# Sparse attention with a soft mixture of experts: three of four q/k strips loaded in 1 KB rows by one transfer each, and a new order of steps

## The chip, the cores and the metric

The kernel runs on one core of one Trainium2 chip. The metric is device time in microseconds (us). Before the change three runs gave 279.32, 279.91 and 282.58 us; the median is 279.91 us. The profiled execution is one more run, at 283.02 us. Granted TensorE clock is given as a share of 2.4 GHz; 0.5 means 1.2 GHz.

## The reference

Eight batches, eight heads, 576 tokens, head size 64, all float32. Heads 0 to 3 see a window of 32 tokens ("local"), heads 4 to 7 the tokens with the same position modulo 32 ("strided"). The attention's output, with heads side by side, goes through a soft mixture of 8 experts with 4 slots each.

```python
mask_local = (rel >= 0) & (rel < 32)
mask_strided = (rel >= 0) & (pos[None, :] % 32 == pos[:, None] % 32)
scores = np.where(masks[None], q @ k.transpose(0, 1, 3, 2) / np.sqrt(D), -1e9)
attn_out = softmax(scores) @ v                   # [8, 8, 576, 64]
x = attn_out.transpose(0, 2, 1, 3).reshape(4608, 512)
logits = x @ phi                                 # [4608, 32]
slot_input = softmax(logits, axis=0).T @ x       # [32, 512]
slot_out[e] = relu(slot_input[e] @ w1[e]) @ w2[e]
out = softmax(logits, axis=1) @ slot_out
```

## The kernel before

**Stages.** The kernel has an attention loop of 16 steps, then a drain and the tail. Step `i` treats batch `i // 2`, and in it two local heads (suffix L) and two strided heads (suffix S). The tail brings in what is left of the expert weights, runs the experts, and stores the output.

**Loads of a step.** Queries and keys of the tokens 64 to 575 come as four strips, kL, qL, kS and qS, each of two heads, 256 KB. `emit_D` issues them on SP's queue. The strip qL is one transfer (line 290): partition p holds four tokens of each head, so that a packet is 1 KB and all 128 partitions are written. The strips kL, kS and qS are two transfers of 128 KB each (line 294): a head has 64 partitions, and each partition holds eight tokens, a packet of 2 KB. The first 64 tokens of all heads (`Dt`, line 299, every second step) and the values (`Dv`, lines 304 and 307, and `Ds`, line 312) are further transfers. Of the 64 blocks of expert weights (512 KB each, line 244 and others) 30 are issued inside the loop (`w`).

**Buffers.** `nat` gives a strip its place: four slots of `natb`, used in turn in the canonical order kL, qL, (t), kS, qS. A load must therefore wait until the load four places earlier has been read by TensorE (or by POOL, which reads qL). The values of the strided heads, `vs`, have one buffer.

**DMA lanes.** The transfers on SP take eight completion semaphores in turn. Each transfer waits until the one eight places before it has landed, so no more than eight are under way.

**Transposes.** `turn` (line 328) transposes four blocks of 128 columns of a strip on TensorE into a PSUM bank, and `emit_e` copies the bank to the tiles `kLb`, `kSb` or `qtb` on ScalarE, with an access pattern that puts tokens in order. For qL, POOL first sorts the strip into `nat2` (`emit_g`, line 323), so that a block holds both heads. In kL, kS and qS a block is a pair of tokens by 64 dimensions, for both heads.

**Order.** Every step has a name (`TkL` transposes kL, `ekL` copies it out, `SL` and `SS` are scores, `a`, `m`, `b`, `EX`, `s` the softmax, `P` and `f` its transposition, `AL` and `AS` the products with values, `X`, `x`, `LG` the later parts) and a number in the table `PHASE`. Step `n` of `i` is emitted at `10 * i + PHASE[n]`; all are sorted by this, and each engine runs its own in that order. Suffixes y and z give numbers of their own to the first and the last `i`.

Of the kernel before, what the change touches and what calls it, by code (L numbers as in the profile page):

```python
# [25 lines left out]
TN = 4  # L26
NI = 36
# [3 lines left out]

PER = 10.0
PHASE = dict(
    Tt=0.3822, et=1.7933, kcL=2.2893, kcS=4.2207, gqL=0.1069, TkL=-4.3302, ekL=-0.8212, TqL=0.1189, eqL=2.3418,
    TkS=0.0364, ekS=4.2997, TqS=1.7301, eqS=2.355, SL=3.2822, SS=6.7794, a2=11.0625, aA=7.9078, a1=7.1235, m2=12.4254,
    m1=8.3441, b2=12.5475, b1=9.6628, EX2=14.022, EX1=11.0057, PA=14.416, fA=16.5383, PL=13.9339, fL=17.5174,
    s2=14.5712, s1=16.4348, rc=17.1249, PS=15.0921, fS=16.9509, AL=19.132, AA=22.0385, nA=23.9111, nL=21.817,
    AS=18.6462, nS=20.038, XS=21.78, xS=23.3769, XL=23.6524, xL=25.5687, XB=24.899, xB=27.8377, LG=27.6985,
    lc=29.6796, T9=24.5604, x9=25.9634, G9=27.1881, lg=29.1761, c9=28.3874, bm=29.2468, ED=29.6763, E9=30.4064,
    EA=29.7637, DT=31.1019, dt=31.2401, zz=32.7907, z9=34.5183, SI=31.8402, S9=32.9908, ac=33.8253, Dt=-4.4167,  # L40
    DkL=-9.127, DqL=-5.5006, DkS=-6.0373, DqS=-4.2053, C2=15.0077, Dv=6.1895, Ds=13.7301, zv=6.3414, SI0=1321.5679,
    S90=1379.9589, SI1=1483.7422, S91=1849.8957, mt=1013.1477, gm=1105.8595, wP=1174.6367, wD=1189.6775, wA=1214.8774,
    zD=1813.3179, zP=2101.5254, rg=2466.7324, ac0=1559.8399, ac1=1877.0405, ms=806.9735, sP0=1634.1847, sD0=1697.2594,
    sP1=2131.0366, sD1=2592.0768, Px=1984.3327, P0=2005.0906, P1=2790.0989, P2=3007.9876, P3=3368.8942, P4=3371.9343,
    P5=3376.775, P6=3689.0133, Dsz=7.9979, DkLz=-6.1029, TkLz=-0.7073, ekLz=3.1899, DqLz=-2.2526, gqLz=3.4277,
    TqLz=7.3306, eqLz=11.7249, DkSz=-8.1864, TkSz=3.3797, ekSz=11.8909, DqSz=-2.1099, TqSz=0.552, eqSz=13.2762,
    kcLz=11.4872, kcSz=10.0958, Dvz=6.9716, C2z=22.07, SLz=12.2707, SSz=13.3533, PAz=288.7773, PLz=321.7366,
    PSz=332.7395, ALz=375.9609, AAz=370.9401, ASz=519.1193, XSz=707.4419, XLz=681.9619, XBz=879.7536, LGz=878.9582,
    T9z=542.7143, G9z=780.8206, DTz=1138.1211, a1z=27.7962, aAz=61.8185, a2z=97.8287, m1z=168.544, m2z=240.9994,
    b1z=208.4859, b2z=261.8524, s1z=294.2249, s2z=308.0275, rcz=328.4212, nSz=697.2792, nLz=530.3168, nAz=475.5805,  # L50
    lgz=900.9235, c9z=787.6677, bmz=934.8942, zzz=1638.7908, z9z=1684.8229, dtz=1148.8275, EX1z=232.6822,
    EX2z=295.8221, fAz=353.4314, fLz=373.5109, fSz=464.8821, xLz=790.8422, xSz=825.6899, xBz=1452.5598, x9z=753.5728,
    EDz=951.8699, E9z=1093.3994, EAz=1408.0027, b9=29.2094, U9=31.8282, u9=32.068, b9z=859.2151, U9z=1267.3242,
    u9z=1341.0063, sw=1523.0731, DkLy=0.0, TkLy=4.4344, ekLy=6.2962, DqLy=-1227.8995, gqLy=-1040.3093, TqLy=-785.3182,
    eqLy=-726.4301, DkSy=-652.0224, TkSy=-612.1271, ekSy=-108.6268, DqSy=-568.916, TqSy=-177.1509, eqSy=-41.0303,
    Dty=-856.1564, Tty=-773.837, ety=-262.108, kcLy=-40.1673, kcSy=-257.5721, Dvy=3.2651, Dsy=8.1858, C2y=15.6738,
    SLy=6.2994, SSy=5.8701, PAy=15.183, PLy=16.1105, PSy=12.2748, ALy=22.3281, AAy=19.7659, ASy=19.3498, XSy=21.7384,
    XLy=25.1438, XBy=26.4902, LGy=28.9777, a1y=9.6423, aAy=8.0076, a2y=6.401, m1y=10.5053, m2y=7.5658, b1y=11.8225,
    b2y=8.6715, s1y=15.3267, s2y=13.3513, rcy=17.4693, nSy=20.9998, nLy=22.8474, nAy=24.2303, EX1y=13.9196,
    EX2y=10.8774, fAy=17.2098, fLy=18.5321, fSy=18.2348, xLy=27.1116, xSy=24.1831, xBy=30.3395, lcy=31.6159, Dw=12.0,  # L60
    Dx=148.0,
)

SEQ = "eehhllllllllsrtrorrorrorrstOOOfff"
# [26 lines left out]
def tile_sparse_attention_soft_moe(  # L91
# [39 lines left out]
    kLb, kSb = big("kLb", 2 * S), big("kSb", 2 * S)  # L131
# [26 lines left out]
    kt = {"kL": kLb, "kS": kSb, "qL": qtb[:, 0:512], "qS": qtb[:, 512:1024]}  # L158
# [18 lines left out]
    x9 = x9b.rearrange("p (c d) -> p c d", c=4)  # L177
# [20 lines left out]
    def give(t):  # L198
# [166 lines left out]
    def emit_kc(s, i):  # L365

        for a in range(2):
            h = slice(64 * a, 64 * a + 64)
            src = tl[h, i % 2 + (2 if s == "S" else 0), 0]
            PC(out=kL[h, a, 0:64] if s == "L" else kA[h, a], in_=src)  # L370
            if s == "S":
                for n in range(2):
                    dst = kSb[64 * n:64 * n + 64].rearrange("d (j h m x) -> d j h m x", h=2, m=2, x=2 * NI)[:, :, a, :, NI * n:NI * n + 4]
                    PC(out=dst, in_=src.rearrange("d (i m j n) -> d j m i n", i=4, m=2, n=2)[:, :, :, :, n])

    def score(t, c, x, wd, lhsT, rhs):
        nc.tensor.matmul(out=t[0][32 * c:32 * c + 32, x:x + wd], lhsT=lhsT, rhs=rhs, start=True, stop=True, skip_group_check=True)  # L377
# [20 lines left out]

    def part(t, which):
# [279 lines left out]
    for s in "LS":  # L679
# [168 lines left out]
    for a in range(2):  # L848
        r = slice(64 - 64 * a, 128 - 64 * a)
# [181 lines left out]
```

## Time and profile before

| | |
|---|---|
| median of three runs | 279.91 us |
| profiled execution | 283.02 us, of which the span from the first to the last instruction is 281.2 us |
| TensorE (PE) busy | 229.4 us, 82% of the span |
| VectorE (DVE) busy | 168.5 us, 60% |
| ScalarE (ACT) busy | 154.0 us, 55% |
| GpSimd (POOL) busy | 83.3 us, 30% |
| DMA | 72.80 MB, mean 259 GB/s; the main queue's packets fill 89.7% of the 16 engines' time |
| chain that ended last | PE 40%, DMA 34%, SP's queue 10% |

Busy times of TensorE are modelled from pipelined matmuls and say little about how much room it has; the gaps between its instructions say more. DMA share is the mean busy share of the 16 DMA engines. The chain is followed back from the last instruction, at each step to what released it. "SPq" is SP's queue issuing a transfer.

### The profile page before, as it was taken

Reading aid. Unit: us, or ns where it says so; the run is one execution under the profiler, and the core shown is the slowest. Engines: PE = TensorE matmul, PEld = TensorE weight load, DVE = VectorE, ACT = ScalarE, POOL = GpSimd, SP = SyncE. Lnnn points to the kernel's source line nnn. Section 1 sums busy time; section 2 is a strip of 40 time slices with the busy share of each in tenths; the row PEclk is TensorE's granted clock in tenths of the full one; section 3 lists DMA queues with packets and bytes.
Section 4 is the critical chain, followed back from the end, with each engine's and each line's share of the span. In section 5 each row is a group of like instructions: output and inputs, shape, how many; then the busy total and the mean of one; then the engine's idle time right before and its main releaser. Section 6 shows DMA issues by size and latency. Waiting matters only on the chain.

```text
span 281.2 us, 9759 instructions
## 1 busy us (share of the span) xinstructions
PE 229.4 (82%) x3974; PEld 173.1 (62%) x3974; DVE 168.5 (60%) x376; ACT 154.0 (55%) x342; POOL 83.3 (30%) x187
## 2 busy tenths in 40 slices
PE   7967797969889597979995999949888999898600
PEld 3755676758668486957983988839674335455400
DVE  5166756865687577668972787845867731035700
ACT  2575847759666665955984598635642114034600
POOL 5262452515246042414705331435210200000000
PEclk9999999999999999998996899987999999999965
DMA  7779999899888999999979968993899999988996
GB/s 180 183 233 235 253 233 239 260 206 281 211 240 228 224 268 226 230 267 260 226 226 243 242 193 250 258 266 95 294 377 393 362 409 325 280 277 288 340 291 264
DMA packets 64813, 72.80 MB, mean 259 GB/s; under 512 B 34048, under 2 KB 48768, under 8 KB 64768
## 3 DMA queue, kind: packets, MB, share of 16 engines
q1 hardware_dynamic: 63808, 71.85, 89.7%
q8 instruction: 31, 0.51, 0.8%
q10 hardware_dynamic: 960, 0.33, 0.6%
q14 instruction: 14, 0.11, 0.2%
HBM read 62.72 MB, written 9.44 MB: 257 GB/s over the span
## 4 chain that ended last, share of the span: by engine, by line
PE 40%; DMA 34%; SPq 10%; issue 4%; DVE 4%; ACT 1%; POOL 1%; DVEq 0%; POOLq 0%; ACTq 0%
DMA natb<-in_q_dram 14%; DMA wb<-in_moe_w_dram 12%; PE bank L328 6%; PE bank L459 5%; DMA vs<-in_v_dram 5%; PE bank L807 4%; PE bank L507 4%; SPq L294 4%; PE bank L377 4%; PE bank L649 3%; PE bank L922 3%; DMA natb<-in_k_dram 2%; PE bank L451 2%; PE bank L947 2%; SPq L304 1%
## 5 line engine op out<-in xcount | busy, mean ns | idle before, releaser
L328 PE MATMUL bank<-cf,natb 128*128 128x128 f32 x280 | 43.7, 291 | 18.4 <-DMA natb<-in_q_dram 8.5
L328 PEld LDWEIGHTS bank<-cf,natb 128*128 128x128 f32 x280 | 31.9, 147 | 29.0 <-issue 8.9
L416 DVE TENSOR_TENSOR pb<-bank,cb 128x288 f32<-128x288 f32 (+2 forms) x48 | 22.6, 474 | 21.7 <-PE bank L377 16.7
L323 POOL COPY natb<-natb 128x512 f32<-128x512 f32 x16 | 9.9, 619 | 80.8 <-DMA natb<-in_q_dram 42.1
L489 DVE TENSOR_TENSOR xnb<-bank,rz 128x512 f32<-128x512 f32 (+1 forms) x33 | 22.0, 669 | 9.6 <-PE bank L459 9.5
L344 ACT COPY kLb<-bank 64x256 f32<-64x256 f32 x64 | 25.3, 395 | 2.6 <-PE bank L377 1.3
L377 PE MATMUL bank<-kLb,qtb 128*32 128x128 f32 x576 | 25.5, 281 | 0.0
L459 PE MATMUL bank<-vs,ptb 128*32 128x128 f32 x480 | 16.4, 274 | 10.5 <-DMA vs<-in_v_dram 5.8
L428 ACT ACTIVATE pb<-pb 128x288 f32<-128x288 f32 (+1 forms) x32 | 19.2, 599 | 7.7 <-DVE pb L424 7.1
L424 DVE TENSOR_TENSOR pb<-pb,mx 128x288 f32<-128x288 f32 (+1 forms) x32 | 22.1, 692 | 0.9
L421 DVE TENSOR_REDUCE mx<-pb 128x8 f32<-128x288 f32 (+1 forms) x32 | 21.8, 681 | 0.6
L431 DVE TENSOR_REDUCE rz<-pb 128x8 f32<-128x288 f32 (+1 forms) x32 | 20.6, 685 | 2.2 <-ACT pb L428 1.7
L507 PE MATMUL bank<-cf,xnb 128*128 128x128 f32 x128 | 21.6, 297 | 0.0
L455 ACT COPY ptb<-bank 128x512 f32<-128x512 f32 x32 | 17.4, 589 | 6.6 <-PE bank L451 5.3
L377 PEld LDWEIGHTS bank<-kLb,qtb 128*32 128x32 f32 x576 | 18.0, 113 | 4.6 <-issue 3.4
L459 PEld LDWEIGHTS bank<-vs,ptb 128*32 128x32 f32 x480 | 13.2, 109 | 12.3 <-ACT kLb L344 4.8
L451 PE MATMUL bank<-cf,pb 128*128 128x128 f32 x128 | 19.6, 278 | 0.0
L351 ACT COPY kSb<-bank 64x512 f32<-64x512 f32 x32 | 18.4, 575 | 1.5 <-PE bank L328 1.1
L318 POOL COPY vb<-vb 64x1024 f32<-64x1024 f32 x16 | 16.6, 1037 | 8.0 <-DMA vb<-in_v_dram 2.7
L459 PE MATMUL bank<-vb,ptb 128*32 128x128 f32 x512 | 17.8, 273 | 0.1
L507 PEld LDWEIGHTS bank<-cf,xnb 128*128 128x128 f32 x128 | 15.9, 152 | 2.5 <-DVE x9b L499 1.0
L338 ACT COPY qtb<-bank 128x512 f32<-128x512 f32 x16 | 9.4, 587 | 14.4 <-PE bank L328 14.4
(173 smaller groups left out, 468.5 us busy)
## 6 DMA issues: line engine op xcount, KB each, us to landing
wb<-in_moe_w_dram SPq DMA_DIRECT2D x48, 512.0 KB
natb<-in_k_dram SPq DMA_DIRECT2D x70, 128.0 KB
natb<-in_q_dram SPq DMA_DIRECT2D x38, 128.0 KB
vb<-in_v_dram SPq DMA_DIRECT2D x32, 144.0 KB
vs<-in_v_dram SPq DMA_DIRECT2D x30, 144.0 KB
natb<-in_q_dram SPq DMA_DIRECT2D x16, 256.0 KB
out_dram<-wb SPq DMA_DIRECT2D x16, 256.0 KB
vb<-in_moe_w_dram SPq DMA_DIRECT2D x4, 512.0 KB
```

Source lines behind the costliest of these rows:

```text
L328: nc.tensor.transpose(out=t[0][:, 128 * n:128 * n + 128], in_=src[:, 128 * n:128 * n + 128], identity=ident)
L344: ACT(out=dst.rearrange("d (p j n) -> d p j n", j=4, n=2)[:, :, :, n], in_=t[0][64 * n:64 * n + 64].rearrange("d (j h p) -> d p j h", j=4, ...
L377: nc.tensor.matmul(out=t[0][32 * c:32 * c + 32, x:x + wd], lhsT=lhsT, rhs=rhs, start=True, stop=True, skip_group_check=True)
L416: nc.vector.tensor_tensor(out=dst, in0=src, in1=mk.rearrange("p (s k) -> p s k", s=n).unsqueeze(3).to_broadcast([P, n, kk, 2]), op=ALU.add)
L421: nc.vector.tensor_reduce(out=part(box[i][0], w), in_=psg[w].rearrange("p s k a -> p s a k"), op=ALU.max, axis=AX.X)
L424: nc.vector.tensor_tensor(out=psg[w], in0=psg[w], in1=over(box[i][0], w), op=ALU.subtract)
L428: nc.scalar.activation(out=t, in_=t, func=AF.Exp, scale=0.125)
L431: nc.vector.tensor_reduce(out=part(box[i][1], w), in_=psg[w].rearrange("p s k a -> p s a k"), op=ALU.add, axis=AX.X)
L451: nc.tensor.transpose(out=t[0][:, 128 * r:128 * r + 128], in_=pb[:, lo + 128 * r:lo + 128 * r + 128], identity=ident)
L459: nc.tensor.matmul(out=t[0][32 * c:32 * c + 32, 128 * r:128 * r + 128], lhsT=lhsT, rhs=rhs, start=True, stop=True, skip_group_check=True)
L489: nc.vector.tensor_tensor(out=xn[:, place(i, s), r0:r0 + nr].rearrange("p r (a d) -> p r a d", a=2), in0=t[0][:, 128 * r0:128 * r0 + 128 * ...
L507: nc.tensor.transpose(out=t[0][:, 128 * r:128 * r + 128], in_=xn[:, place(i, s), r, :], identity=ident)
```

## The change

The three strips kL, kS and qS get the layout of qL: partition p holds four tokens of each of both heads, in packets of 1 KB over all 128 partitions, and one transfer of 256 KB brings them. Their blocks of 128 columns are now pairs of tokens of one head; nothing is sorted, and the copies out of PSUM, the small copies of `emit_kc` and the index in `emit_SS` follow the new places. The strip qL still goes through POOL's sort. All numbers of the table `PHASE` are new.

```diff
-    Tt=0.3822, et=1.7933, kcL=2.2893, kcS=4.2207, gqL=0.1069, TkL=-4.3302, ekL=-0.8212, TqL=0.1189, eqL=2.3418,
+    Tt=-2.0579, et=-0.6655, kcL=0.1445, kcS=1.0426, gqL=-4.396, TkL=-6.6862, ekL=-3.8918, TqL=-3.1071, eqL=-1.5805,
...
         src = (k if x[0] == "k" else q)[i // 2, heads(i, x[1]), 64:]
-        if x == "qL":
-            nc.sync.dma_start(out=nat(x, i).rearrange("p (h x) -> p h x", h=2), in_=src.rearrange("h (p n) d -> p h (n d)", n=TN))
-        else:
-
-            for h in range(2):
-                nc.sync.dma_start(out=nat(x, i)[64 * h:64 * h + 64], in_=src[h].rearrange("(p n) d -> p (n d)", n=8))
+        nc.sync.dma_start(out=nat(x, i).rearrange("p (h x) -> p h x", h=2), in_=src.rearrange("h (p n) d -> p h (n d)", n=TN))
...
-                    ACT(out=dst.rearrange("d (p j n) -> d p j n", j=4, n=2)[:, :, :, n],
-                        in_=t[0][64 * n:64 * n + 64].rearrange("d (j h p) -> d p j h", j=4, h=2)[:, :, :, a])
+                    ACT(out=dst.rearrange("d (p j n) -> d p j n", j=2, n=2)[:, :, :, n],
+                        in_=t[0][64 * n:64 * n + 64].rearrange("d (h j p) -> d p j h", j=2, h=2)[:, :, :, a])
         elif x == "qS":
-            ACT(out=kt[x].rearrange("d (x m i) -> d x m i", m=2, i=32), in_=t[0].rearrange("d (x i m) -> d x m i", i=32, m=2))
+
+            ACT(out=kt[x].rearrange("d (x m i) -> d x m i", m=4, i=32), in_=t[0].rearrange("d (x i m) -> d x m i", i=32, m=4))
...
-                    y = 2 * c + z
-                    x = 4 * (y % 4) + 2 * h + y // 4
+                    x = 8 * h + 4 * z + c
                     score(t, c, 128 + 2 * NI * (2 * h + z), 2 * NI, kt["qS"][:, 32 * x:32 * x + 32], kSb[:, 2 * NI * x:2 * NI * x + 2 * NI])
```

SP's queue, from the values of group 4 to a weight block, in the kernel before. Line 312 is `Ds4`, line 294 with `in_k` is kS of group 6, line 290 its qL, line 299 the first tokens, line 294 with `in_q` its qS, line 304 `Dv5`. The words in brackets are what the transfer waits for; "DMAHW" with a number is a lane.

```order
L312 DMA vs<-in_v_dram 36x1024 [waits DMAHW7_49,PE_49]
L312 DMA vs<-in_v_dram 36x1024 [waits DMAHW0_49]
L294 DMA natb<-in_k_dram 64x512 [waits DMAHW1_49,PE_49]
L294 DMA natb<-in_k_dram 64x512 [waits DMAHW2_49]
L290 DMA natb<-in_q_dram 128x2x256 [waits DMAHW3_49,Pool_49]
L299 DMA natb<-in_k_dram 64x8x64 [waits DMAHW4_49]
L299 DMA natb<-in_q_dram 64x8x64 [waits DMAHW5_49]
L294 DMA natb<-in_q_dram 64x512 [waits DMAHW6_49,PE_49]
L294 DMA natb<-in_q_dram 64x512 [waits DMAHW7_49]
L304 DMA vb<-in_v_dram 64x9x64 [waits DMAHW0_49]
L304 DMA vb<-in_v_dram 64x9x64 [waits DMAHW1_49]
L244 DMA wb_96<-in_moe_w_dram 128x1024 [waits DMAHW2_49]
```

The same place of SP's queue after the change, one group of strips later in the list (group 7: kL, `Ds5`, a weight block, then qL, kS and qS, then `Dv6`). Line 288 is a whole strip.

```order
L288 DMA natb<-in_k_dram 128x2x256 [waits DMAHW6_49,Pool_49]
L306 DMA vs<-in_v_dram 36x1024 [waits DMAHW7_49,PE_49]
L306 DMA vs<-in_v_dram 36x1024 [waits DMAHW0_49]
L243 DMA wb_97<-in_moe_w_dram 128x1024 [waits DMAHW1_49]
L288 DMA natb<-in_q_dram 128x2x256 [waits DMAHW2_49]
L288 DMA natb<-in_k_dram 128x2x256 [waits DMAHW3_49]
L288 DMA natb<-in_q_dram 128x2x256 [waits DMAHW4_49,PE_49]
L298 DMA vb<-in_v_dram 64x9x64 [waits DMAHW5_49,PE_49]
L298 DMA vb<-in_v_dram 64x9x64 [waits DMAHW6_49]
```

A strip is one row instead of two, so the lanes come round after fewer strips; qL now stands ahead of kS, and `Ds` ahead of the weight block that it followed.

TensorE's order in the middle of a step before the change, from the transposition of qS (line 328) over `XS` (507), `SI` (649), `AA` (459), `SL` (377), `XL` (507), `PL` (451), `PA` (440), `XB` (528) and `PS` (451) to that of the next kL.

```order
L328 MATMUL bank_124<-cf,natb 128x128 x4
L507 MATMUL bank_120<-cf,xnb 128x128 x4
L649 MATMUL bank_121<-xnb,dt 32x256 x8
L459 MATMUL bank_119<-vb 32x128 x4
L377 MATMUL bank_117<-kLb,qtb 32x128 x16
L507 MATMUL bank_122<-cf,xnb 128x128 x4
L451 MATMUL bank_123<-cf,pb 128x128 x4
L440 MATMUL bank_124<-cf,pb 128x128
L528 MATMUL bank_120<-cf,xtb 128x128 x4
L451 MATMUL bank_121<-cf,pb 128x128 x4
L328 MATMUL bank_119<-cf,natb 128x128 x4
```

The same stretch after the change; 501 is now the line of `XS` and `XL`, 322 of the strips, 643 of `SI`, 453 of `AA`, 372 of `SL`, 445 of `PL` and `PS`, 522 of `XB`, 434 of `PA`.

```order
L501 MATMUL bank_118<-cf,xnb 128x128 x4
L322 MATMUL bank_123<-cf,natb 128x128 x4
L643 MATMUL bank_120<-xnb,dt 32x256 x8
L453 MATMUL bank_124<-vb 32x128 x4
L372 MATMUL bank_121<-kLb,qtb 32x128 x16
L445 MATMUL bank_119<-cf,pb 128x128 x4
L501 MATMUL bank_117<-cf,xnb 128x128 x4
L445 MATMUL bank_122<-cf,pb 128x128 x4
L522 MATMUL bank_118<-cf,xtb 128x128 x4
L322 MATMUL bank_120<-cf,natb 128x128 x4
L434 MATMUL bank_124<-cf,pb 128x128
```

The same instructions stand in both; neighbours have changed places: qS after `XS`, `PL` ahead of `XL`, `PS` ahead of `XB`, `PA` behind the next kL.

## Rows read from the trace of the kernel before

**Rows 1.** Windows: stretch, its length, busy us per engine, clock, DMA share, GB/s.

```profile
20.00:180.00 160.00, 137.67 (x2721) 116.27 (x2722) 112.08 (x248) 110.05 (x247) 62.60 (x145) 0.97 0.95 239
180.00:200.00 20.00, 16.35 (x315) 14.17 (x317) 12.29 (x27) 10.54 (x24) 8.36 (x14) 0.83 0.73 199
200.00:232.00 32.00, 28.73 (x351) 14.71 (x343) 21.60 (x59) 9.13 (x22) 2.93 (x3) 1.00 0.99 381
```

**Rows 2.** Chain that ended last, from 20 to 190 us, shares by line.

```profile
by line: DMA natb<-in_q_dram 19.2%; DMA wb<-in_moe_w_dram 12.7%; PE bank L328 8.6%; DMA vs<-in_v_dram 7.5%; PE bank L459 6.2%; PE bank L377 5.9%; PE bank L507 5.6%; issue 4.8%; SPq L294 4.5%; DMA natb<-in_k_dram 4.1%; PE bank L649 3.9%; PE 
```

**Rows 3.** Pieces of that chain and of its start: start us, length us, what.

```profile
12.56 3.16 DMA natb<-in_q_dram
...
39.15 7.34 DMA wb<-in_moe_w_dram
...
51.63 6.69 DMA wb<-in_moe_w_dram
...
87.89 7.63 DMA wb<-in_moe_w_dram
95.58 0.50 SPq L294
```

**Rows 4.** TensorE's timeline over two steps: start, us, operation, idle time before it.

```profile
88.87 1.06 PE L377 MATMUL bank<-kLb,qtb 128*32 128x128 f32 x32
...
96.79 1.08 PE L459 MATMUL bank<-vs,ptb 128*32 128x128 f32 x32 [3.14 <-ACT pb L428]
...
100.59 0.63 PE L328 MATMUL bank<-cf,natb 128*128 128x128 f32 x4 [0.28 <-DMA natb<-in_q_dram]
...
108.93 1.08 PE L459 MATMUL bank<-vs,ptb 128*32 128x128 f32 x32 [1.44 <-ACT kLb L344]
...
111.98 1.09 PE L328 MATMUL bank<-cf,natb 128*128 128x128 f32 x8 [0.51 <-POOL natb L323]
...
113.68 1.06 PE L377 MATMUL bank<-kLb,qtb 128*32 128x128 f32 x32
```

**Rows 5.** SP's issues by line: duration ns min/median/max, first and last start.

```profile
L294 SPq DMA_DIRECT2D natb<-in_k_dram x62: 465/594/2179, 5.3 to 177.2; - x62
L290 SPq DMA_DIRECT2D natb<-in_q_dram x16: 427/527/1814, 0.7 to 181.5; - x16
```

**Rows 6.** SP's timeline: start, us for all of a row, transfer.

```profile
0.74 0.45 SPq L290 DMA_DIRECT2D natb<-in_q_dram  x1
...
5.32 3.05 SPq L294 DMA_DIRECT2D natb<-in_k_dram  x4
...
14.29 1.66 SPq L312 DMA_DIRECT2D vs<-in_v_dram  x2
...
226.91 15.48 SPq L256 DMA_DIRECT2D wb<-in_moe_w_dram  x8
```

**Rows 7.** Windows where one kind of transfer runs (columns as in rows 1).

```profile
7.00:9.00 2.00, 2.00 (x9) 1.47 (x9) 0.00 (x0) 0.59 (x1) 0.44 (x3) 1.00 0.93 246
...
236.00:238.00 2.00, 2.00 (x41) 1.23 (x44) 0.43 (x1) 0.61 (x2) 0.00 (x0) 1.00 0.97 326
238.00:240.00 2.00, 2.00 (x44) 1.23 (x40) 0.00 (x0) 0.00 (x0) 0.00 (x0) 1.00 0.99 305
```

**Rows 8.** SP's waits: who waited for whom, us in total, times, longest.

```profile
SPq L294 <- DMA wb<-in_moe_w_dram: 5.5, 5, 1.6
```

**Rows 9.** Groups by line: busy us, mean ns of one, idle us before and who ended it.

```profile
L323 POOL COPY natb<-natb 128x512 f32<-128x512 f32 x16 | 9.9, 619 | 80.8 <-DMA natb<-in_q_dram 42.1 <-PE bank L459 21.2 <-DMA vb<-in_v_dram 6.4
...
L347 ACT COPY qtb<-bank 128x512 f32<-128x512 f32 x16 | 9.5, 592 | 4.3 <-PE bank L328 4.2
L338 ACT COPY qtb<-bank 128x512 f32<-128x512 f32 x16 | 9.4, 587 | 14.4 <-PE bank L328 14.4
```

More of the change, by code (lines that the diff above doesn't have):

```diff
@@ L33 @@
 PHASE = dict(
-    Tt=0.3822, et=1.7933, kcL=2.2893, kcS=4.2207, gqL=0.1069, TkL=-4.3302, ekL=-0.8212, TqL=0.1189, eqL=2.3418,
[L35 to L58, printed above, removed]
@@ L59 @@
-    b2y=8.6715, s1y=15.3267, s2y=13.3513, rcy=17.4693, nSy=20.9998, nLy=22.8474, nAy=24.2303, EX1y=13.9196,
-    EX2y=10.8774, fAy=17.2098, fLy=18.5321, fSy=18.2348, xLy=27.1116, xSy=24.1831, xBy=30.3395, lcy=31.6159, Dw=12.0,
-    Dx=148.0,
+    Tt=-2.0579, et=-0.6655, kcL=0.1445, kcS=1.0426, gqL=-4.396, TkL=-6.6862, ekL=-3.8918, TqL=-3.1071, eqL=-1.5805,
+    TkS=-2.8079, ekS=0.2405, TqS=-1.638, eqS=2.0281, SL=0.8447, SS=4.3002, a2=4.9137, aA=5.6049, a1=4.0131, m2=9.2207,
+    m1=7.9989, b2=10.3387, b1=8.4466, EX2=10.6844, EX1=9.7238, PA=13.5374, fA=17.3669, PL=12.8131, fL=15.0172,
@@ new lines @@
+    s2=12.3728, s1=10.9688, rc=12.5764, PS=12.8393, fS=13.2679, AL=16.6069, AA=20.3205, nA=21.9987, nL=20.3493,
+    AS=15.8184, nS=18.2514, XS=18.3058, xS=21.1039, XL=22.8265, xL=22.9517, XB=23.0972, xB=27.0486, LG=25.4195,
+    lc=28.2806, T9=23.2544, x9=24.5474, G9=25.2863, lg=26.0999, c9=25.9908, bm=26.6978, ED=26.9719, E9=27.6734,
+    EA=28.1908, DT=27.3659, dt=28.3798, zz=29.6743, z9=30.6305, SI=30.0667, S9=30.5273, ac=31.1579, Dt=-5.774,
+    DkL=-9.8545, DqL=-6.5505, DkS=-6.2446, DqS=-5.1332, C2=13.94, Dv=5.3521, Ds=10.9507, zv=9.5434, SI0=1233.6152,
@@ new lines @@
+    S90=1337.0003, SI1=1340.2779, S91=1792.2637, mt=1006.8642, gm=1224.659, wP=1232.9455, wD=1351.0811, wA=1457.2594,
+    zD=1674.8517, zP=2208.5085, rg=3431.8563, ac0=1540.6421, ac1=1908.4892, ms=1369.382, sP0=1599.2965, sD0=1636.4837,
+    sP1=2063.102, sD1=2063.7014, Px=1936.2395, P0=1956.3048, P1=2242.6644, P2=2744.3559, P3=3051.4956, P4=3384.7871,
+    P5=4048.1529, P6=4135.3064, Dsz=10.4973, DkLz=-14.2155, TkLz=-3.0006, ekLz=8.8872, DqLz=1.1442, gqLz=4.0624,
+    TqLz=8.953, eqLz=10.94, DkSz=-10.8748, TkSz=-3.877, ekSz=-1.7646, DqSz=-7.0334, TqSz=1.8577, eqSz=6.1303,
@@ new lines @@
+    kcLz=1.2757, kcSz=0.4144, Dvz=3.6518, C2z=471.0423, SLz=11.0707, SSz=10.5949, PAz=396.9704, PLz=458.8301,
+    PSz=519.4974, ALz=589.7334, AAz=551.4381, ASz=603.3993, XSz=714.4744, XLz=685.0062, XBz=965.6281, LGz=774.6018,
+    T9z=667.5722, G9z=730.2393, DTz=1063.5269, a1z=159.2114, aAz=122.2744, a2z=91.9546, m1z=210.8829, m2z=271.9005,
+    b1z=240.0783, b2z=315.4588, s1z=397.8074, s2z=434.2949, rcz=475.8997, nSz=667.9874, nLz=643.2038, nAz=593.3993,
+    lgz=966.0232, c9z=730.9931, bmz=995.0075, zzz=1381.7738, z9z=1523.0304, dtz=1228.5284, EX1z=327.7961,
@@ new lines @@
+    EX2z=346.6191, fAz=414.1154, fLz=476.6392, fSz=551.6975, xLz=699.8901, xSz=756.0396, xBz=1328.1133, x9z=680.0565,
+    EDz=1017.2556, E9z=1047.5151, EAz=1358.9622, b9=26.413, U9=30.0178, u9=30.0947, b9z=792.3005, U9z=1160.7289,
+    u9z=1264.6704, sw=1495.1309, DkLy=0.0, TkLy=0.282, ekLy=1.1911, DqLy=-1954.5694, gqLy=-1013.5182, TqLy=-708.2666,
+    eqLy=-330.8771, DkSy=-1033.3414, TkSy=-455.8707, ekSy=-317.8524, DqSy=-435.3099, TqSy=-270.9075, eqSy=-233.4198,
+    Dty=-1569.5444, Tty=-714.8319, ety=-474.0413, kcLy=-54.7535, kcSy=-144.5437, Dvy=2.0079, Dsy=0.5923, C2y=14.7865,
@@ L62 @@
+    SLy=4.7404, SSy=0.3891, PAy=13.5974, PLy=13.6588, PSy=10.7209, ALy=18.5353, AAy=16.8047, ASy=16.3107, XSy=21.3403,
+    XLy=26.5822, XBy=26.0313, LGy=29.2819, a1y=8.6685, aAy=8.1403, a2y=1.3758, m1y=9.2843, m2y=5.5075, b1y=9.4624,
+    b2y=6.6793, s1y=11.0301, s2y=13.7963, rcy=14.228, nSy=17.5206, nLy=21.4472, nAy=24.8177, EX1y=9.84, EX2y=7.1264,
+    fAy=15.7781, fLy=15.6772, fSy=12.598, xLy=26.792, xSy=24.9093, xBy=34.1502, lcy=30.3079, Dw=12.0, Dx=148.0,
 )
@@ L350, in emit_e @@
                 r = slice(64 * n, 64 * n + 64)
-                ACT(out=kt[x][r].rearrange("d (x m n i) -> d x m n i", m=2, n=2, i=NI)[:, :, :, n, 4:],
-                    in_=t[0][r].rearrange("d (x i m) -> d x m i", i=32, m=2))
+                ACT(out=kt[x][r].rearrange("d (x m n i) -> d x m n i", m=4, n=2, i=NI)[:, :, :, n, 4:],
+                    in_=t[0][r].rearrange("d (x i m) -> d x m i", i=32, m=4))
         give(t)
@@ L372, in emit_kc @@
                 for n in range(2):
-                    dst = kSb[64 * n:64 * n + 64].rearrange("d (j h m x) -> d j h m x", h=2, m=2, x=2 * NI)[:, :, a, :, NI * n:NI * n + 4]
-                    PC(out=dst, in_=src.rearrange("d (i m j n) -> d j m i n", i=4, m=2, n=2)[:, :, :, :, n])
+                    dst = kSb[64 * n:64 * n + 64].rearrange("d (h j m x) -> d h j m x", h=2, m=4, x=2 * NI)[:, a, :, :, NI * n:NI * n + 4]
+                    PC(out=dst, in_=src.rearrange("d (i m j n) -> d j m i n", i=4, m=4, n=2)[:, :, :, :, n])
     def score(t, c, x, wd, lhsT, rhs):
```

## Prediction

> **What bounds the kernel now.** I read the windows by stage first. From 20 to 180 us the 16 DMA engines are 0.95 busy and yet move only 239 GB/s, while the same engines carry 381 GB/s from 200 to 232 us, where only weight blocks run [rows 1]. So the loop keeps the queues full with transfers that go slowly. In the chain of waits inside the loop (20 to 190 us, 170 us long) the four DMA entries make 19.2 + 12.7 + 7.5 + 4.1 = 43.5%, 74 us, and SP's issuing at line 294 another 4.5%, 7.7 us [rows 2]. No engine alone is the bound: TensorE's timeline shows why. From one `SL` to the second next one, 88.87 to 113.68 us, two steps take 24.8 us, 12.4 each, and the gaps before instructions add up to 3.14 + 0.28 + 1.44 + 0.51 = 5.4 us [rows 4]. TensorE's own work is thus 19.4 us, 9.7 a step; 2.7 us a step are waits. SP is nearly as full: a step has 14.9 issues on average (k and q strips 7, values 4, first tokens and their values 2, weights 30/16 = 1.9), and at 0.53 to 0.59 us each [rows 5] that is 8 to 9 of 12.4 us. The loop is a coupling of three nearly full resources, and the transfers are the slowest of them.
>
> After the loop the weight stretch is DMA at 0.99 [rows 1]. Its blocks wait for buffers that the last steps set free, so it starts when the loop ends and keeps its length; what the loop gains, the end gains.
>
> **The change, part by part.**
>
> *Rate of the strips.* Of the 64 strips 48 change layout. Between 7 and 9 us the queues carry nearly nothing but strips in halves (the four halves issued from 5.32 us on, and those ahead of them [rows 6]), at 0.93 share and 246 GB/s [rows 7]: 262,144 bytes take 1.07 us. Packets of 1 KB over all partitions run alone from 236 to 240 us, the last weight blocks, issued at line 256 [rows 6], at 326 and 305 GB/s [rows 7]: 0.83 us. That is 0.235 us saved per strip. Five strips lie in the start-up; 43 x 0.235 = 10.1 us of queue time in the loop. How much of it reaches the end? All, if the queues bind everywhere: −10.1. If only the part of the chain that runs through DMA shrinks, 43.5%: −4.4. The share of 0.95 speaks for the first, the 57% of the chain outside DMA for the second; neither is nearer, so I take the middle, **−7.3**.
>
> The Trainium skill speaks on both sides here. Its page "DMA: Bandwidth & Descriptors", section "Why small descriptors are slow (HBM only)", has a fixed overhead of about three cycles for each packet, against 32 bytes a cycle: 1 KB rows would then cost 70 cycles where 2 KB rows cost 67. By that rule alone the strips would get 4.5% slower, 43 x 1.07 x 0.045 = +2 us (an estimate from that page). The windows show the contrary sign, 326 and 305 against 246 GB/s, so the width of the transfer outweighs its packet size; the sum goes by the windows.
>
> *Issues.* 96 issues at 594 ns become 48 at 527 ns, the price of the form that qL has had [rows 5]: 31.7 us less of SP's time. Most of it lies beside full queues. On the chain SP's line 294 has 7.7 us from 20 to 190 us [rows 2]. A pair of 2 x 0.594 us becomes one of 0.527 us [rows 5], so at most 55% goes, −4.3; nothing, if the queues would have held the next transfer anyway. I take **−2.1**.
>
> *Start-up.* The chain begins with SP alone: the first issue is at 0.74 us [rows 6], and qL of group 1 is issued at 12.56 us [rows 3] as the 18th. It becomes the 14th: six issues fewer (a second half of each of the first four strips, and both halves of kS, which now follows), 6 x 0.594 = 3.6 us, but `Ds0` is moved ahead of it, 1.66 us for its two issues [rows 6]. **−1.9**.
>
> *Lanes.* Three pieces of the chain, 7.34, 6.69 and 7.63 us, are a weight block's flight, and when the third ends SP issues again [rows 3]: that is the wait for the lane eight issues back, of which SP shows 5.5 us at this line alone [rows 8]. Eight issues are now 8/14.9 of a step, 6.7 us; with 11.9 issues to a step they are 8.3 us. The block has 1.6 us more to land: at most 3 x 1.6 = −4.9, nothing if SP runs ahead to fill them. I take **−2.4**.
>
> *qL ahead of kS.* POOL waits 42.1 us for qL [rows 9], because kS, ahead of it on SP, waits for the previous qS to be transposed. Now qL goes out without that wait, and kS takes its place as the last strip, to be transposed after it. What is late next is kS, without the 0.62 us of sorting behind it. I count 0: the gain is in the queue's term already. Behind a qS that waits for the next kL (even groups, before and after alike) stand `Dv`, a weight block and the next kL.
>
> *Copies.* The same number of transposes and of elements. Copies with another stride cost the same already: 592 ns with pairs (line 347), 587 with groups of four (line 338) [rows 9]. The moved `PL`, `PS`, `XL`, `XB` and `PA` are cheap to misplace: between `AS` of the group before, which starts `nS`, `b` and `EX` on the way to `PL`, and `PL` itself TensorE has `AL`, three strips, `XS`, `AA` and `SL` as cover. 0; with that cover gone, a gap like the 1.44 us of [rows 4] in every second step, +11.
>
> *Sum.* −1.9 −7.3 −2.1 −2.4 = −13.7. The profiled execution, 281.2 us of span and 1.8 around it, goes from 283.0 to 269.3; it lies 3.1 above the median of 279.9, which goes to **266.2 us**. With all lower ends −6.3, 273.6 us; with all upper ends −21.2, 258.7 us.
>
> **Rivals.**
>
> *More than that (chance 0.13).* The strips run as fast as the weight blocks do, 381 GB/s [rows 1], 0.69 us each, and every term comes in full: 43 x 0.38 = 16.3, with 4.3, 4.9 and 1.9 a sum of −27.4, **252.5 us**. TensorE would not forbid it, with 2.7 us a step to give. For it: a strip in halves writes 64 partitions at a time. Against: 1 KB packets alone reached 305 to 326. The page "SBUF — State Buffer" of the Trainium skill, section "Door 1: The DMA port swizzle", would have it so: partitions 0 to 63 reach 8 of 16 ports, half of 435 GB/s; by it a whole strip could take 0.60 us (an estimate from that page). The row's 246 GB/s is near that half, with the next transfer in the other half of the partitions overlapping.
>
> *Hidden (0.20).* The gaps of TensorE [rows 4] are filled from elsewhere: single `vs`, four slots, a softmax chain that sets the pace in the second half, where DMA share falls to 0.73 from 180 us [rows 1]. Only the start-up remains: 279.9 − 1.9 = **278.0 us**.
>
> *Slower (0.12): a deeper queue.* Eight lanes hold 8/14.9 of a step's 12.4 us x 239 GB/s = 2.96 MB, 1.59 MB, which takes 6.7 us. With 11.9 issues they hold 1.99 MB, 8.3 us, a quarter more. If SP, with time to spare, keeps all eight lanes filled, every load lands a quarter later, and the 74 us of DMA on the chain become 92.5: +18.5, less 7.3 and 1.9, **289.2 us**. It decides when SP waits mostly for lanes; now that is 5.5 us at the line that issues most strips [rows 8], and the four slots hold the strips back before the lanes do. Both speak against it.
>
> **How the numbers follow.** Forecast 0.55, more 0.13, hidden 0.20, slower 0.12. A difference of 2% (5.6 us) is about what a measurement of this kernel can tell from no change. The forecast's own range, 259 to 274, lies below 274.3 and counts as faster, as does the first rival: 0.68 faster, 0.20 the same, 0.12 slower. The range that leaves out the slower case and the end of the first rival is 253 to 280 us.
>
> **What would show it.** In the profile after: 64 issues of 256 KB near 0.53 us; a rate above 239 GB/s in the loop, near 255, with the share still above 0.85; POOL's wait for qL far below 42 us; steps near 11.5 us; a weight stretch of the same length that starts some 12 us earlier. The rate term is wrong if the loop's rate stays at 239 GB/s while its share does; the order is at fault if share and rate both fall and TensorE's gaps name ACT or DVE; the deeper queue is right if SP's waits for lanes grow.

## The result, and the profile after

The changed kernel takes 253.21 us (median of four runs, 251.09 to 258.89); the kernel before, run again beside it, 281.13 us. The ratio is 0.8985, with a 95% interval of 0.8882 to 0.9087: 10% faster, 28 us, twice what was forecast. Times here and below are medians of all runs of a kernel; the ratios leave out runs more than 1.5% above the fastest of the same kernel, and where no interval is given only one run was within that. The profiled execution after is 253.95 us, its span 252.1 us.

Windows of the profile after, with the columns of [rows 1]:

```profile
20.00:180.00 160.00, 151.74 (x3195) 133.16 (x3188) 131.11 (x293) 126.15 (x282) 73.79 (x160) 0.99 0.96 282
...
180.00:200.00 20.00, 18.37 (x156) 8.17 (x157) 12.33 (x39) 4.50 (x13) 1.85 (x2) 0.91 0.90 344
```

Against [rows 1] the queues are as busy from 20 to 180 us, 0.96 after 0.95, but move 282 instead of 239 GB/s; by 180 us the loop is over and the weight stretch runs.

The chain that ended last, whole span, by engine, and then its lines from 20 to 170 us:

```profile
PE 75%; DMA 8%; DVE 4%; issue 3%; ACT 2%; SPq 1%; POOL 0%; DVEq 0%
```

```profile
by line: PE bank L322 18.9%; PE bank L453 18.3%; PE bank L372 14.5%; PE bank L445 8.8%; PE bank L501 7.9%; PE bank L643 4.7%; DMA natb<-in_k_dram 4.2%; PE bank L533 4.1%; PE bank L522 3.8%; issue 2.2%; DMA vb<-in_v_dram 1.8%; PE bank L562 1
```

In [rows 2] the four DMA entries held 43.5% of the loop's chain; now the two that the line still lists hold 6%. The loop runs from one product on TensorE to the next. Its timeline between two `SL` (line 372 now) shows the same:

```profile
99.90 1.06 PE L372 MATMUL bank<-kLb,qtb 128*32 128x128 f32 x32
...
120.84 1.06 PE L372 MATMUL bank<-kLb,qtb 128*32 128x128 f32 x32
```

Two steps take 20.9 us, where [rows 4] had 24.8 with 5.4 us of gaps; between these two rows the timeline lists no gap of TensorE at all.

SP's issues of the whole strips (line 288), durations ns min/median/max as in [rows 5]:

```profile
L288 SPq DMA_DIRECT2D natb<-in_q_dram x31: 368/415/1443, 0.7 to 160.5; - x31
L288 SPq DMA_DIRECT2D natb<-in_k_dram x31: 367/413/1837, 4.0 to 150.1; - x31
```

A whole strip costs 0.41 us of SP's time, where two halves cost 2 x 0.594; even the form that existed before, 0.527 us for qL, has become shorter.

The tail moved as a block. The first product of the experts' first layer, after and then before:

```profile
190.09 1.50 PE L801 MATMUL bank<-wb,pb 128*32 128x512 f32 x12
```

```profile
217.57 1.92 PE L807 MATMUL bank<-wb,pb 128*32 128x512 f32 x16
```

It starts 27.5 us earlier, and the span is 29.1 us shorter: nearly all the gain lies ahead of the weight stretch, in the loop.

### The profile page after: what moved, and what is told of

The parts are those of the page before. It is cut to its first block, busy times and chain, and to the rows that moved or that the text cites. A ratio compares the mean times of both kernels' runs of the same rounds, so it can differ in the third digit from the quotient of the medians.

```text
span 252.1 us, 9686 instructions
## 1 busy us (share of the span) xinstructions
PE 219.6 (87%) x3974; PEld 170.4 (68%) x3974; DVE 165.9 (66%) x376; ACT 154.5 (61%) x342; POOL 85.1 (34%) x187
## 4 chain that ended last, share of the span: by engine, by line
PE 75%; DMA 8%; DVE 4%; issue 3%; ACT 2%; SPq 1%; POOL 0%; DVEq 0%
PE bank L322 13%; PE bank L453 12%; PE bank L372 9%; PE bank L445 6%; PE bank L916 6%; PE bank L801 6%; PE bank L501 5%; PE bank L643 4%; DMA natb<-in_k_dram 2%; PE bank L533 2%; PE bank L522 2%; PE bank L941 2%; DMA natb<-in_q_dram 2%; DMA xnb<-in_q_dram 2%; PE bank L562 1%
## 5 line engine op out<-in xcount | busy, mean ns | idle before, releaser
L322 PE MATMUL bank<-cf,natb 128*128 128x128 f32 x280 | 41.4, 281 | 8.2 <-DMA xnb<-in_q_dram 3.3
L410 DVE TENSOR_TENSOR pb<-bank,cb 128x288 f32<-128x288 f32 (+2 forms) x48 | 21.3, 473 | 20.6 <-ACT kLb L338 11.0
L338 ACT COPY kLb<-bank 64x256 f32<-64x256 f32 x64 | 26.1, 408 | 2.5 <-PE bank L372 1.3
L317 POOL COPY natb<-natb 128x512 f32<-128x512 f32 x16 | 10.1, 631 | 44.2 <-DMA natb<-in_q_dram 35.3
L425 DVE TENSOR_REDUCE rz<-pb 128x10 f32<-128x640 f32 (+1 forms) x32 | 21.8, 686 | 3.7 <-ACT pb L422 3.1
L453 PE MATMUL bank<-vb,ptb 128*32 128x128 f32 x512 | 19.0, 283 | 0.3 <-issue 0.3
L453 PE MATMUL bank<-vs,ptb 128*32 128x128 f32 x480 | 17.2, 273 | 2.3 <-ACT lall L538 1.5
L501 PE MATMUL bank<-cf,xnb 128*128 128x128 f32 x128 | 19.2, 273 | 0.0
L312 POOL COPY vb<-vb 64x1024 f32<-64x1024 f32 x16 | 17.3, 1078 | 4.0 <-DMA vb<-in_v_dram 2.1
L365 POOL COPY kLb<-qtb 64x64 f32<-64x64 f32 x32 | 7.9, 247 | 29.2 <-ACT qtb L357 28.2
L313 POOL COPY vb<-vb 64x1024 f32<-64x1024 f32 x16 | 17.0, 1064 | 0.7
L369 POOL COPY kSb<-qtb 64x32 f32<-64x32 f32 x64 | 16.2, 253 | 2.3
```

Of the source, the lines that this page charges most:

```text
L322: nc.tensor.transpose(out=t[0][:, 128 * n:128 * n + 128], in_=src[:, 128 * n:128 * n + 128], identity=ident)
L338: ACT(out=dst.rearrange("d (p j n) -> d p j n", j=2, n=2)[:, :, :, n], in_=t[0][64 * n:64 * n + 64].rearrange("d (h j p) -> d p j h", j=2, ...
L410: nc.vector.tensor_tensor(out=dst, in0=src, in1=mk.rearrange("p (s k) -> p s k", s=n).unsqueeze(3).to_broadcast([P, n, kk, 2]), op=ALU.add)
L425: nc.vector.tensor_reduce(out=part(box[i][1], w), in_=psg[w].rearrange("p s k a -> p s a k"), op=ALU.add, axis=AX.X)
L453: nc.tensor.matmul(out=t[0][32 * c:32 * c + 32, 128 * r:128 * r + 128], lhsT=lhsT, rhs=rhs, start=True, stop=True, skip_group_check=True)
L501: nc.tensor.transpose(out=t[0][:, 128 * r:128 * r + 128], in_=xn[:, place(i, s), r, :], identity=ident)
```

## Experiments

Three theories were set against each other. *Width*: a transfer that writes only the upper or lower 64 partitions is slow. *Issues*: SP's time per issue, and the eight lanes, keep the queues from being filled. *Order*: the new table takes waits away.

**Order or layout.** `order_alone` is the kernel before with the new table:

```diff
-    Tt=0.3822, et=1.7933, kcL=2.2893, ...
+    Tt=-2.0579, et=-0.6655, kcL=0.1445, ...
```

> The kernel before with the new table PHASE and nothing else: strips kL, kS and qS still in two transfers over 64 partitions, 2 KB packets. Theory 'width' (transfers over all partitions run faster and the loop was held by their rate) expects 275 to 285 us, a loop rate near 240 GB/s. Theory 'issues' (fewer issues on SP and fewer lanes used) expects the same, 275 to 285 us. Theory 'order' (qL ahead of kS, values ahead of weights, other neighbours) expects most of the 28 us: 255 to 262 us.

Measured: 281.97 us, ratio to the kernel before 0.9988 (0.9933 to 1.0043). The order alone is worth nothing. `layout_alone` is the other half, the kernel after with the old table (the same diff, reversed).

> The kernel after with the old table PHASE: whole strips in 1 KB packets over 128 partitions, one transfer each, in the old order. 'Width' and 'issues' expect most of the gain: 254 to 262 us, loop rate 270 GB/s or more. 'Order' expects 272 to 282 us.

Measured: 254.78 us (median of four, no interval). The layout alone gives 26 of the 28 us. Theory *order* is out, in both layouts.

**One transfer or two, and which partitions.** Three runs cut the strips kL, kS and qS of the kernel after in two transfers of 128 KB again, in three ways. `two_by_head`:

```diff
-        nc.sync.dma_start(out=nat(x, i).rearrange("p (h x) -> p h x", h=2), ...)
...
+            for h in range(2):
+                nc.sync.dma_start(out=nat(x, i)[:, 256 * h:256 * h + 256], in_=src[h].rearrange("(p n) d -> p (n d)", n=TN))
```

> The kernel after, but kL, kS and qS go in two transfers again, one per head: each over all 128 partitions in 1 KB packets, 128 KB. Packets, their places and their width are those of after; the issues and the lanes used are those of before. 'Width' expects 252 to 258 us and a loop rate above 270 GB/s. 'Issues' expects 264 us or more and SP waiting for lanes again.

Measured: 264.94 us, ratio 0.9392 (0.9327 to 0.9456). `two_by_partitions` cuts at partition 64 instead:

```diff
...
+            for g in range(2):
+                nc.sync.dma_start(out=nat(x, i)[64 * g:64 * g + 64].rearrange("p (h x) -> p h x", h=2),
+                                  in_=src[:, 256 * g:256 * g + 256].rearrange("h (p n) d -> p h (n d)", n=TN))
```

> The kernel after, but kL, kS and qS go in two transfers, one per half of the partitions: 64 partitions, both heads, 1 KB packets, 128 KB each. Same bytes, packets, issues and lanes as with two transfers by head; only the width of one transfer differs. 'Width' expects a clear loss against that run: 265 us or more, a loop rate near 245 GB/s. 'Issues' expects the same time as that run, within 2%.

Measured: 286.28 us, ratio 1.0121 (1.001 to 1.0231): the whole gain is gone. `two_by_parity` sends even and odd partitions (`nat(x, i)[g::2]`), again 64 partitions and 128 packets to a transfer.

> The kernel after, but kL, kS and qS go in two transfers, one for the even and one for the odd partitions: 64 partitions, both heads, 1 KB packets, 128 KB, as in the run with two transfers by halves of the partitions; only the set of 64 partitions differs. If the upper or lower half of the partitions is what is slow (fewer ways into the memory), 262 to 268 us, as with two transfers by head (264.9), loop rate above 255 GB/s. If 64 partitions to a transfer are slow whichever they are, 280 us or more.

Measured: 272.76 us (median of four, 267.87 to 275.02, no interval). Between 286.28 and 272.76 us nothing differs but the set of 64 partitions, and with it the rows of memory that a transfer reads; `spread_before`, below, leaves the rows as they were. The slowest of the four runs is 8.2 us under the fastest with halves, 283.22 us. So 64 partitions are not slow as such; a contiguous half is, by 13.5 us between the medians. The median is above the 262 to 268 expected, where only the fastest run lies; what follows shows where the rest may lie.

The window from 20 to 160 us tells the two effects apart. First the kernel before, then `two_by_partitions`, `two_by_parity`, `two_by_head` and the kernel after:

```profile
20.00:160.00 140.00, 118.02 (x2342) 99.17 (x2346) 95.75 (x209) 93.52 (x210) 53.76 (x126) 0.96 0.97 241
```

```profile
20.00:160.00 140.00, 116.69 (x2395) 99.11 (x2395) 96.26 (x212) 97.21 (x215) 54.16 (x125) 1.00 0.96 236
```

```profile
20.00:160.00 140.00, 124.79 (x2598) 109.26 (x2598) 104.08 (x228) 105.26 (x233) 59.76 (x134) 0.99 0.86 253
```

```profile
20.00:160.00 140.00, 129.18 (x2684) 112.40 (x2682) 107.36 (x240) 108.40 (x243) 60.21 (x139) 0.99 0.90 261
```

```profile
20.00:160.00 140.00, 133.48 (x2849) 117.88 (x2845) 115.74 (x258) 113.50 (x253) 66.17 (x153) 1.00 0.97 279
```

Divide the last column by the one before it. With halves of the partitions a busy queue moves 241/0.97 = 248 and 236/0.96 = 246 GB/s; without them 253/0.86 = 294, 261/0.90 = 290 and 279/0.97 = 288. (In `order_alone`, also with halves, it is 239/0.93 = 257.) Contiguous halves set the rate of a busy queue; among the three without them, the number of issues, and perhaps their price, sets how busy it is, 0.86 and 0.90 against 0.97.

**Width alone, in the kernel before.** `spread_before` gives each head of kL, kS and qS every second partition and leaves transfers, packets of 2 KB, lanes and order as they were (the copies out of PSUM follow the new places, which the cut diff does not show):

```diff
-                nc.sync.dma_start(out=nat(x, i)[64 * h:64 * h + 64], in_=src[h].rearrange("(p n) d -> p (n d)", n=8))
+                nc.sync.dma_start(out=nat(x, i)[h::2], in_=src[h].rearrange("(p n) d -> p (n d)", n=8))
...
```

> The kernel before, old order, two transfers per strip of one head each, 64 partitions and 2 KB packets, but a head takes every second partition instead of a half of them (the copies follow the new places). Issues, lanes, packets and bytes are those of before. 'Width' expects most of what issues leave of the gain: 260 to 268 us and a loop rate above 255 GB/s. 'Issues' and 'packet size' expect 277 us or more.

Measured: 269.96 us, ratio 0.9675 (0.9558 to 0.9792), a little above the 260 to 268 expected. Its window and its issues:

```profile
20.00:160.00 140.00, 124.50 (x2613) 108.58 (x2614) 102.76 (x229) 103.47 (x232) 58.70 (x134) 0.99 0.87 257
```

```profile
L294 SPq DMA_DIRECT2D natb<-in_k_dram x62: 472/594/1657, 5.3 to 165.3; - x62
```

257/0.87 = 295 GB/s for a busy queue, the fast level, but a queue that is busy only 0.87: SP still spends 0.594 us on each of twice as many issues.

The trace also has the size and the duration of every packet, and they say who pays for the halves. These are means over the packets that start between 20 and 160 us, in the kernel before and in `spread_before`: 133 and 107 ns for 2 KB (the three strips), 72 and 54 for 1 KB (qL), 22.6 and 18.0 for 256 bytes (first tokens and `Dv`), 213 and 200 for 4 KB (weights and `Ds`). In the kernel after, whose queues are as full as those of the kernel before, 1 KB takes 54 ns, 256 bytes 19.0 and 4 KB 202, so it is not that a fuller queue is slower. The halves thus slow what runs beside them too. With the packet counts of the kernel before the differences add up to 19.9 us on each of the 16 engines, 7.3 of the strips and 12.6 of their neighbours.

In `two_by_head` an issue of the same size is shorter:

```profile
L292 SPq DMA_DIRECT2D natb<-in_k_dram x62: 327/404/1377, 5.2 to 159.4; - x62
L292 SPq DMA_DIRECT2D natb<-in_q_dram x30: 333/376/1231, 14.2 to 163.3; - x30
```

The 64-partition issues of `two_by_partitions` take 612 ns:

```profile
L292 SPq DMA_DIRECT2D natb<-in_k_dram x62: 595/612/1502, 5.5 to 178.8; - x62
```

Those of `two_by_parity` take 607 ns at the median, so which 64 partitions they write makes no difference to SP's price. The price may be the reason for the 7.8 us between the medians of `two_by_parity` and `two_by_head`; but their runs overlap (267.87 to 275.02 and 263.59 to 268.53 us), and no run changes the price alone. What sets it is open too: qL, in one form throughout, costs 527 ns in the kernel before and 420 in `two_by_partitions`, and a weight block over 128 partitions costs 586 ns inside the loop of the kernel before and 383 behind it.

**The number of issues alone.** `tiny_after` is the kernel after with a transfer of 64 bytes behind each of the 48 strips:

```diff
+        if x != "qL":
+            tn[0] += 1
+            nc.sync.dma_start(out=tiny[0:16, tn[0] % 8:tn[0] % 8 + 1], in_=cfd[0:16, 0:1])
```

> The kernel after with a transfer of 64 bytes (16 partitions, 4 bytes each) behind each of the 48 whole strips of kL, kS and qS. SP issues as many transfers and passes as many lanes as in the kernel before, and no strip changes. If the number of issues and lanes makes the 12 us between one whole strip (253.2 us) and two transfers by head (264.9): 261 to 268 us. If the smaller size of a transfer does: 255 us or less.

Measured: 264.66 us, ratio 0.9357 (0.9291 to 0.9424), the same as `two_by_head` (0.9392). 48 more issues that carry nothing cost 11.5 us; that strips are cut in two costs nothing more that can be told.

An issue costs SP time, and it occupies a lane. From 20 to 160 us SP's issues take 114 us in the kernel after, 121 in `tiny_after`, 116 in `two_by_head`, 125 in `spread_before` and 126 in `two_by_parity`; its waits that the profile puts down to a landing, which frees a lane, are 3.7, 6.0, 9.6, 1.3 and 1.1 us. All such waits of `spread_before`:

```profile
SPq L304 <- DMA wb<-in_moe_w_dram: 1.3, 2, 0.9
```

So in the two runs with every second partition it is SP's own time that is short, and hardly the lanes; with transfers by head the lanes have a larger part.

**Taking issues from SP.** Weight blocks of the loop were moved to other queues; POOL's has eight lanes of its own, ACT's shares those of SP. In four kernels all 30 moved, to POOL's queue in three and to ACT's in `w_act_after`:

```diff
-                nc.sync.dma_start(out=buf, in_=w1[...])
+                (nc.gpsimd if len(wts) <= NWBUF else nc.sync).dma_start(out=buf, in_=w1[...])
```

> The kernel before, but the 30 weight blocks of the loop are issued from POOL's queue instead of SP's (bytes, packets and order otherwise the same). SP has two issues of about 0.59 us less per step, 12% of its loop time, and the blocks no longer take SP's lanes. If SP's issuing is hidden behind the slow halves in the kernel before: 276 to 285 us. If SP's issuing or the lanes already set the pace there: 268 us or less.

Measured: 277.11 us, ratio 0.9892 (0.9549 to 1.0235): no difference that can be told. From 20 to 160 us its queues are 0.98 busy and still move only 237 GB/s.

> The kernel before with each head on every second partition (269.96 us), and the 30 weight blocks of the loop issued from POOL's queue. In that run SP issues for 125 of the 140 us from 20 to 160 us. If SP's time is what separates it from the kernel after: 256 to 263 us. If something else does (the number of transfers itself, packet size): 267 us or more.

Measured: 266.68 us, ratio 0.9586 (0.9348 to 0.9823), less than *issues* expected. From 160 to 180 us its queues are busy 0.62, against 0.84 in `spread_before`: the loop's end had become slower.

> The kernel after with the 30 weight blocks of the loop issued from POOL's queue. If SP still holds it up (114 of 140 us in the same stretch): 245 to 250 us. If TensorE sets the pace, or POOL's queue is late with qL: 251 to 257 us.

Measured: 254.93 us, ratio 0.916 (0.8951 to 0.9369): nothing gained.

> The kernel after with the 30 weight blocks of the loop issued from ACT's queue. ACT gets two issues a step, some 0.4 us each, and waits in order for lanes. If SP holds the kernel after up, 247 to 252 us; if ACT's copies then come late for TensorE, 255 us or more.

Measured: 265.32 us (median of four, no interval), slower than the kernel after: even its fastest run takes 260.4 us. From 20 to 160 us SP waits 27.5 us for the landing of weight blocks, which ACT now sends, against 2.8 in the kernel after; they hold lanes that SP's next transfers need.

Then only the first 24 blocks went to POOL's queue (`len(wts) <= 24`), and the loop's end was left alone.

> Two transfers per strip by head (264.9 us), with the first 24 weight blocks issued from POOL's queue; the last six stay on SP, away from the end of the loop. SP loses 24 issues and 24 lanes of the 48 that the halving adds. If issues and lanes are what the halving costs: 255 to 260 us. If not: 263 us or more.

Measured: 260.26 us, ratio 0.9195 (0.912 to 0.927), against 0.9392 without the move. Half of the added issues are gone, and 4.7 of the 11.7 us with them, a little less than was expected.

> The kernel before with each head on every second partition (269.96 us), the first 24 weight blocks from POOL's queue. If issues and lanes hold it: 257 to 263 us, with 265 to 275 GB/s from 20 to 160 us. If not: 267 us or more.

Measured: 264.66 us, ratio 0.9362 (0.9282 to 0.9441), against 0.9675. The windows of these two runs, by head and spread:

```profile
20.00:160.00 140.00, 135.34 (x2822) 118.53 (x2821) 115.42 (x254) 113.30 (x252) 76.03 (x171) 0.99 0.94 273
```

```profile
20.00:160.00 140.00, 129.11 (x2697) 112.22 (x2687) 108.99 (x242) 108.68 (x245) 71.94 (x166) 1.00 0.90 269
```

The share rises, 0.90 to 0.94 and 0.87 to 0.90, and the rate of a busy queue stays, 290 and 299 GB/s. Both runs agree in sign with *issues*, though both gained somewhat less than it expected.

> The kernel after with the first 24 weight blocks from POOL's queue. If SP's issues and lanes still cost it something: 247 to 251 us, faster than the kernel after. If TensorE sets its pace: 252 to 256 us.

Measured: 255.29 us, ratio 0.8991 (0.8894 to 0.9088), equal to the kernel after.

```profile
20.00:160.00 140.00, 134.56 (x2875) 118.60 (x2877) 115.89 (x258) 113.80 (x254) 78.67 (x177) 1.00 0.99 283
```

The kernel after has no use for a freer SP. No version has a lower median.

**Is TensorE the new bound?** The transposes of `XB` were made twice, in both kernels:

```diff
-            nc.tensor.transpose(out=t[0][:, 128 * r:128 * r + 128], in_=xt_tile("S", r), identity=ident)
+            for _ in range(2):
+                nc.tensor.transpose(out=t[0][:, 128 * r:128 * r + 128], in_=xt_tile("S", r), identity=ident)
```

> The kernel before with the same doubling, 7.0 us more of TensorE's work. If transfers set the pace of its loop, 279 to 284 us (0 to 3 us more); if TensorE does, 286 us or more.

Measured: 280.2 us, ratio 1.0019 (0.9964 to 1.0074): 7 us of work cost nothing, TensorE had the room.

> The kernel after with the four transposes of XB made twice in each of the 16 steps, 0.44 us more of TensorE's work a step, 7.0 us in all; results unchanged. If TensorE now sets the pace of the loop: 257 to 262 us. If the loop still waits for transfers: under 256 us.

Measured: 254.81 us, ratio 0.9126 (0.8983 to 0.9269), against 0.8985 (0.8882 to 0.9087) without. The intervals overlap. The step from the ratios, 1.4% or 4 us of the 7, is not clear of noise; that TensorE sets the pace now rests on the chain and the timeline, and this run leaves it open. The rival is the queues themselves, busy 0.97 in the kernel after and 0.99 in `w24_pool_after`: both may be nearly full at once.

## Why the prediction was wrong

The sign, the mechanism and the place were right; the size was not, 28 us for 13.7. Two steps failed: the terms for issues and lanes were far too small, and the rate term let only the strips become faster. The medians of the runs in the new order add up, from the kernel with the new table and the old strips to the kernel after: 281.97 to 286.28 us (packets of 1 KB instead of 2 KB, still in halves, +4.3; the intervals of the two ratios overlap); to 272.76 (the set of partitions, −13.5); to 264.94 (all 128 partitions to a transfer, −7.8); to 253.21 (one transfer instead of two, −11.7). Between the fastest runs the four steps are +5.1, −15.4, −4.3 and −12.5, so the third is the least certain. The steps were measured in three sets, in which the kernel before has medians from 280.7 to 282.4 us.

- **Rate of the strips**, forecast −7.3, at most −10.1. Width measured −13.5 from halves to every second partition; with the +4.3 of the shorter packets the term's own net is −9.2. In the kernel before, width was worth 0.9675, 9 us, though SP's issues held it back there. So the term belonged at its upper end or above. The price of a strip was right: 0.235 us were forecast, and 26 ns on each of its 128 packets of 2 KB are 0.21 us over 16 engines. The failing step is that nothing else was to become faster, with the loop's rate near 255 GB/s. The loop reached 282, and a busy queue, at 242 to 257 GB/s with halves in any run, reached 286 or more: the packets beside the strips were slowed by the halves too, and their 12.6 us between 20 and 160 us are more than the 7.3 of the strips. The middle between "all" and "the chain's share" was the wrong choice as well: a share of 0.95 meant that the queues bound everywhere.
- **The rival "more than that"** gave 252.5 us, close to the 253.2 that came, but the agreement of the sum is luck: its 1.9 us of start-up did not come, its 9.2 us for issues and lanes were too little, and a busy queue reached 286 or more and not the 381 GB/s that it gave the strips. Its mechanism, contiguous halves that are slow as such, is what `two_by_parity` against `two_by_partitions` shows. This is the rule of the Trainium skill, page "SBUF — State Buffer", section "Door 1: The DMA port swizzle", by which partitions 0 to 63 reach half of the ports; the 13.5 us agree with it.
- **Packets.** The rule weighed against the change (Trainium skill, "DMA: Bandwidth & Descriptors", "Why small descriptors are slow (HBM only)") has the sign of the first step above, +4.3 us where the estimate was +2; that step is barely clear of noise, and the two runs also differ in the heads that share a transfer. The prediction's comparison of windows mixed width and packet size and so saw only the sum.
- **Issues and lanes**, forecast −2.1 and −2.4, at most −9.2 together. `tiny_after` makes the number alone 11.5 us, and the price of one issue may be the cause of 4 to 8 more. This is the step that failed most. It counted line 294 on the chain, 4.5% [rows 2]. The chain probably put SP's lateness down to DMA: a transfer that was sent late looks there like a transfer that is slow. SP's issuing was the better sign, and the prediction had that too low as well, 8 to 9 of 12.4 us a step. It priced all issues like strips, but those of `Dv` and `Ds` cost 0.64 and 0.77 us at the median; from 20 to 160 us the trace of the kernel before has 115 us of issuing, 10.2 in 12.4. In the kernel before the slow halves hid it (`w_pool_before`), and once they are gone it is the next bound.
- **Start-up**, forecast −1.9, did not come. SP's timeline after:

```profile
5.16 2.81 SPq L306 DMA_DIRECT2D vs<-in_v_dram  x2
...
13.08 0.38 SPq L288 DMA_DIRECT2D natb<-in_q_dram  x1
```

  qL of group 1 is the 14th issue, as said, but it goes out at 13.08 us instead of 12.56 [rows 3]: `Ds0` took 2.81 us, not 1.66, and SP then waits 2.3 us for a slot of `natb` that TensorE is still reading.
- **qL ahead of kS**, counted 0, was right in effect: the order alone is worth nothing. POOL's wait for qL was to fall far below 42 us and fell to 35.3. It seems to have cost nothing, for POOL is 0% of the chain above and TensorE had other work:

```profile
L317 POOL COPY natb<-natb 128x512 f32<-128x512 f32 x16 | 10.1, 631 | 44.2 <-DMA natb<-in_q_dram 35.3 <-DMA vb<-in_v_dram 4.9 <-PE bank L434 4.0
...
L342 ACT COPY qtb<-bank 128x512 f32<-128x512 f32 x16 | 9.5, 593 | 0.1
L332 ACT COPY qtb<-bank 128x512 f32<-128x512 f32 x16 | 9.4, 584 | 12.3 <-PE bank L322 12.2
```

- **Copies**, counted 0, was right: 593 and 584 ns against 592 and 587 in [rows 9].
- **The deeper queue** did not come. SP waits for buffers now, not for lanes:

```profile
SPq L288 <- PE bank L434: 6.4, 5, 1.6
SPq L288 <- PE bank L453: 5.8, 8, 1.5
```

- **Left open.** SP's time for an issue and the lane that it occupies were always changed together; what tells them apart here is SP's waits alone.

## What to carry to other kernels

Look at the set of partitions that a transfer writes before its packet size: loads in two contiguous halves of them took about a seventh of the rate of the whole mix, most of it from the transfers beside them. Then read DMA share and rate together: a share near 1 at a low rate asks for other transfers, a share well below 1 for fewer or cheaper issues. Count an issuing queue's own time per step as one counts an engine's; the chain of waits may show its lateness as slow DMA.

## What was not expected of the hardware

SP's time to issue a transfer of 128 KB was 0.61 us over 64 partitions and 0.38 to 0.40 us over 128, with 1 KB packets in both; a whole strip of 256 KB took 0.41 us. The number of partitions is not all of it: the 64 bytes over 16 partitions of `tiny_after` took 0.46 us. And a queue whose transfers all went to scattered or to all partitions moved 286 to 301 GB/s when busy in every run, whatever the packets of the strips were, 1 or 2 KB; one with contiguous halves in it 242 to 257. The halves slowed even packets of 256 bytes that do not belong to them, from 18.0 to 22.6 ns.
